# Pooled attention and expert routing on one core: GpSimd's gathers held by one-element copies, weight loads and transposes placed elsewhere in the order

## The chip, the cores and the metric

The kernel runs on one core of one Trainium2 chip. A core has TensorE (PE in the profile), VectorE (DVE), ScalarE (ACT), GpSimd (POOL) and SyncE (SP), each with its own instruction queue, worked off in order. Sixteen DMA engines move data between the off-chip memory and the on-chip buffers; in this kernel GpSimd and SyncE issue all transfers. The metric is the device time of one execution in microseconds (us). Four executions of the kernel before took 259.3, 260.16, 262.19 and 262.2 us; their median is 261.17 us.

## The reference

```python
# q, k, v: (8, 8, 576, 64) f32;  domain_id: 4608 ids of 8 experts;  w1: (8, 512, 1024), w2: (8, 1024, 512) f32
k_p = k.reshape(B, H, 72, 8, D).mean(axis=3);  v_p = v.reshape(B, H, 72, 8, D).mean(axis=3)
attn = softmax(q @ k_p.T / sqrt(D));           x = (attn @ v_p)     # heads joined: x is (4608, 512)
for e in range(8):
    mask = domain_id == e
    out[mask] = np.maximum(x[mask] @ w1[e], 0) @ w2[e]
```

Keys and values are averaged over groups of eight positions, each query attends to the 72 averages, and each of the 4608 resulting rows of 512 numbers goes through the two-layer network of the one expert that its id names.

## The kernel before, in words

**Attention.** The eight batches are worked in four pairs, 0 to 3. For each pair `load_pair` brings in k, q and v (one GpSimd DMA each, f32 in memory and f16 on chip, two buffers per kind). TensorE pools and turns them (`kp_units`, `qt_units`, `vp_units`), `sc_unit` makes the scores of one batch and head (ScalarE takes their exponential out of PSUM), and `av_unit` makes 128 rows of x, which VectorE divides into `x_sb`. After every third `av_unit`, SyncE stores 384 KB of x into the DRAM tensor `x_lin`; there are twelve such stores, three per pair.

**Routing.** In the shadow of the attention the kernel sorts the tokens: each expert has 640 slots, five blocks of 128. `xrow` holds, per slot, the row of `x_lin` to fetch. `gather(e, j)` is one indirect GpSimd DMA of 128 rows into block j of `xg[e % 2]`. For experts 0 and 1 the first three blocks (384 slots, "early") hold only tokens of pairs 0 to 2, so they can be gathered before pair 3 is done; blocks 3 and 4 ("late") need pair 3's rows too.

**Experts.** `turn_units` transposes gathered blocks on TensorE, two blocks at a time, and VectorE copies them to `xT`. `l1_units` gives the eight units of a first layer (ReLU by ScalarE and VectorE in turn, into `hT`), `l2_units` one unit per block of the second layer; each of these ends with a copy to `y` and an indirect GpSimd DMA that scatters 128 rows to `out`. `wload_units(e, which, 1)` is one GpSimd DMA of 2 MB of f32 weights (1 MB on chip): w1 if `which` is 0, w2 if it is 1. Weights of experts 0, 1, 5 and 6 have buffers of their own; the others take the buffers of q, k and v.

**What sets the order.** The order on every engine is written out by hand. While pair p is in work, `put` gives each unit a number, and the list `plan`, sorted by it, is run; 16 numbers make one pair, so pair 3 has 48 to 64. After the plan the calls stand in the order of the code from line 732 on, and `merge` spreads one list between the units of another. [...] GpSimd carries all loads, gathers and scatters in one queue; the framework gives its DMAs eight completion semaphores in rotation, so each DMA on that queue also waits until the one issued eight before it has landed. `nc.values_load` has every engine read the number of overflow blocks into a register, for a branch after the last expert (tokens beyond 640 per expert; there are none in this data).

The names that the change touches: `load_pair` (line 107), the copy after a turned q (493), the plan's weight loads, gathers and turns (710 to 726), the order of the experts (732 to 772). The loads of expert e's two weights are called w1[e] and w2[e] below.

Of the kernel before, what the change touches and what calls it, by code (L numbers as in the profile page):

```python
# [8 lines left out]
F16 = mybir.dt.float16  # L9
# [8 lines left out]
N = B * S  # L18
FF = 1024
E = 8  # L20
# [3 lines left out]
CAP = 640  # L24
NBL = CAP // 128
NBLK = E * NBL
EARLY = 384
# [12 lines left out]
def kernel(  # L40
# [10 lines left out]
    nc = tc.nc  # L51
    const = ctx.enter_context(tc.tile_pool(name="const", bufs=1))
# [51 lines left out]
            return lambda *a, **kw: self.units.append(lambda: getattr(nc.vector, name)(*a, **kw))  # L104

    x_lin = dram.tile([XROWS, HD], F16, name="x_lin")
    def load_pair(t_ap, pr, tag):
        t = wp.tile([128, 72, D], F16, tag=tag, bufs=2, name=tag)
        nc.gpsimd.dma_start(
            t[:].rearrange("p t d -> p (t d)"),  # L110
            t_ap[2 * pr:2 * pr + 2].rearrange("b h (g t) d -> (b h g) (t d)", g=8))
        return t

    with tc.manual_schedule():
# [447 lines left out]
        def wload_units(e, which, parts):  # L562
            box = {}

            def unit(i):
                if i == 0:
                    tag = W_AT[e][which]
                    bufs = 4 if tag == "w" else 2
                    t = wp.tile([128, 4096] if tag == "w" else [128, 72, D], F16, tag=tag, bufs=bufs, name=tag)
                    box["t"] = t[:] if tag == "w" else t[:].rearrange("p t d -> p (t d)")[:, 0:4096]  # L570
                    if which == 0:
                        box["s"] = moe_w1[e].rearrange("(p k) f -> p k f", k=4)
                    else:
# [4 lines left out]
                nc.gpsimd.dma_start(box["t"][:, n * i:n * i + n], box["s"][:, n * i:n * i + n])  # L578
            return [lambda i=i: unit(i) for i in range(parts)]
# [3 lines left out]
        def gather(e, j, rows=XROWS):  # L583
            i = nc.gpsimd.indirect_dma_start(  # L584
                out=xg[e % 2][:, j, :], out_offset=None, in_=x_lin[0:rows, :],
                in_offset=bass.IndirectOffsetOnAxis(ap=xrow[:, NBL * e + j:NBL * e + j + 1], axis=0),
                bounds_check=rows - 1, oob_is_err=False)
            tc.add_to_no_dep_group("xg", i.ins)
# [129 lines left out]

# [26 lines left out]
        u = l1_units(0, EARLY, CAP, h0, 0)  # L745
        g = [lambda j=j: gather(2, j) for j in range(NBL)]
        run(merge(u[:5], g[:3] + count_b()) + [v[2]] + turn_units(1, 3, NBL) + merge(u[5:], g[3:]))
        nblk = nc.values_load(nblk_i[0:1, 0:1], min_val=0, max_val=N // 128)
        h1 = hidden()
        run(l1_units(1, EARLY, CAP, h1, 0))  # L750
        u = l2_units(0, EARLY, CAP, h0) + l2_units(1, EARLY, CAP, h1)
        t = turn_units(2, 0, NBL)
        run([u[0], wload_units(3, 0, 1)[0], t[0], u[1], t[1], u[2], wload_units(3, 1, 1)[0], t[2], u[3]])
        for e in range(2, E):
            h = hidden()
            u = l1_units(e, 0, CAP, h, 0)
            if e == E - 1:
                nc.gpsimd.drain()
            g = []
            if e + 1 < E:  # L760
                g += [lambda j=j: gather(e + 1, j) for j in range(NBL)]
            if e + 2 < E:
                g += wload_units(e + 2, 0, 1)
            run(merge(u, g))
            u = l2_units(e, 0, CAP, h)
            t = turn_units(e + 1, 0, NBL) if e + 1 < E else []
            if e + 2 < E:
                u = u[:1] + wload_units(e + 2, 1, 1) + u[1:]
            n = len(u)
            for i, f in enumerate(t):  # L770
                u.insert(n - 3 + 2 * i, f)
            run(u)

    main.close()

# [110 lines left out]
```

The softmax here doesn't subtract the row's maximum and nothing guards it: scores larger than these inputs give would overflow.

## Time and profile before

| | |
|---|---|
| four executions, us | 259.3, 260.16, 262.19, 262.2 |
| median | 261.17 |
| the profiled execution | 260.09 |
| its span in the profile | 258.4 |
| TensorE busy | 225.9 (87%) |
| VectorE, ScalarE, GpSimd busy | 121.1, 93.1, 108.6 |
| DMA: moved, mean rate | 50.19 MB, 194 GB/s |
| off-chip memory read, written | 67.15 MB, 15.20 MB |

The span runs from the first to the last instruction of one profiled execution; that execution's own time is 1.7 us longer. Times inside the profile count from the span's start. "L578" is line 578 of the kernel. A slice is a fortieth of the span, 6.46 us. DMA is the mean busy share of the sixteen DMA engines; a share above 1 means that packets overlap on an engine. A name such as `k<-in_moe_w_dram` is a weight load into a buffer of tag "k".

### The profile page before, as it was taken

To read this page: it belongs to the slowest core of one execution; us is meant where nothing else is said; L and a number is where in the kernel's file an instruction comes from. 1 tells how busy PE (TensorE), PEld (TensorE's weight loads), DVE (VectorE), ACT (ScalarE), POOL (GpSimd) and SP (SyncE) were. 2 spreads that over 40 slices of the span, in tenths; PEclk is the share of its full clock that TensorE was granted. 3 is DMA by queue.
4 is the path that set the end of the run, shared out by engine and by line. 5 is a ranking of instruction groups with operands and counts; after the bars stand their busy time and mean duration, and the time that the engine had idled before them with its cause. 6 is when DMAs were issued, how large, how long until landed. Compare 5 with 4: busy or idle time off the path is not lost.

```text
span 258.4 us, 4980 instructions
## 1 busy us (share of the span) xinstructions
PE 225.9 (87%) x2048; PEld 144.7 (56%) x2048; DVE 121.1 (47%) x276; ACT 93.1 (36%) x157; POOL 108.6 (42%) x124
## 2 busy tenths in 40 slices
PE   0777989999878469998959999999999999999990
PEld 0555666677556245555735745755756756656640
DVE  7357499696777244443533234333333333343320
ACT  1045657878667614232310420321312312303210
POOL 7002413320000172048745756665756755643052
PEclk9996799999999657999999999999999999999999
DMA  6999999999999969918997999979989989822032
GB/s 106 214 217 217 215 215 228 244 242 243 242 246 261 204 129 243 241 57 146 239 287 164 204 245 205 274 147 219 283 148 193 257 152 190 263 90 100 3 118 81
DMA packets 18153, 50.19 MB, mean 194 GB/s; under 512 B 2316, under 2 KB 10574, under 8 KB 15568
## 3 DMA queue, kind: packets, MB, share of 16 engines
q0 software_dynamic: 16320, 45.10, 80.7%
q1 hardware_dynamic: 1808, 4.76, 5.0%
q8 instruction: 16, 0.26, 0.4%
q14 instruction: 9, 0.07, 0.1%
HBM read 67.15 MB, written 15.20 MB: 319 GB/s over the span
## 4 chain that ended last, share of the span: by engine, by line
PE 41%; DMA 34%; issue 10%; POOL 6%; DVE 5%; POOLq 1%; ACT 0%; DVEq 0%
DMA v<-in_v_dram 19%; PE big L619 10%; PE small L635 9%; DMA xg<-x_lin,xrow 9%; PE wide L635 5%; PE wide L619 5%; DMA out_dram<-y,tok 4%; POOL out_dram L644 4%; PE small L464 3%; PE turn L598 3%; DMA x_lin<-x_sb 2%; PE big L506 2%; DVE x_sb L532 1%; PE big L526 1%; DVE qT L496 1%
## 5 line engine op out<-in xcount | busy, mean ns | idle before, releaser
L584 POOL DMA_INDIRECT xg<-x_lin,xrow x40 | 41.0, 1026 | 63.7 <-DVE x_sb L532 35.9
L644 POOL DMA_INDIRECT out_dram<-y,tok x40 | 40.1, 1004 | 44.4 <-ACT y L642 22.9
L635 PEld LDWEIGHTS <-hT 128*128 128x128 f16 x272 | 25.9, 98 | 26.7
L509 ACT ACTIVATE at<-big 72x576 f16<-72x576 f32 x44 | 28.2, 645 | 20.0 <-PE big L506 19.1
L619 PEld LDWEIGHTS <-w 128*128 128x128 f16 x256 | 24.6, 99 | 11.9 <-issue 2.2
L625 DVE TENSOR_SCALAR hT<-big 128x640 f16<-128x640 f32 (+1 forms) x21 | 15.3, 729 | 27.7 <-PE big L619 24.6
L619 PE MATMUL big<-xT,w 128*128 128x320 f16 (+2 forms) x172 | 28.2, 309 | 0.0
L599 DVE COPY xT<-turn 128x1024 f16<-128x1024 f16 (+1 forms) x24 | 14.4, 598 | 25.3 <-PE turn L598 25.3
L642 ACT ACTIVATE y<-small 128x512 f32<-128x512 f32 x14 | 8.4, 597 | 42.8 <-PE small L635 40.0
L623 ACT ACTIVATE hT<-big 128x640 f16<-128x640 f32 (+1 forms) x21 | 13.2, 628 | 25.9 <-PE big L619 25.9
L598 PE MATMUL turn<-ident,xg 128*128 128x128 f16 x160 | 14.0, 226 | 8.0 <-DMA xg<-x_lin,xrow 8.0
L598 PEld LDWEIGHTS <-xg 128*128 128x128 f16 x160 | 11.0, 100 | 15.0 <-DMA xg<-x_lin,xrow 10.0
L640 DVE COPY y<-small 128x512 f32<-128x512 f32 x13 | 9.0, 692 | 20.1 <-PE small L635 20.1
L635 PE MATMUL small<-w,hT 128*128 128x512 f16 x72 | 17.0, 379 | 0.0
L526 PEld LDWEIGHTS <-at 72*128 72x128 f16 (+1 forms) x320 | 14.0, 105 | 5.3 <-issue 1.5
L506 PE MATMUL big<-qT,kpT 64*72 64x288 f16 x88 | 14.6, 328 | 2.1 <-DVE qT L496 1.7
L532 DVE TENSOR_TENSOR x_sb<-big,rcp 128x512 f16<-128x512 f32 x23 | 15.9, 691 | 0.8
L619 PEld LDWEIGHTS <-k 128*128 128x128 f16 x128 | 12.5, 98 | 5.2
L509 ACT ACTIVATE at<-wide 72x576 f16<-72x576 f32 x20 | 12.9, 646 | 5.5 <-PE wide L506 5.2
L464 PE MATMUL small<-ident,v 128*128 128x128 f16 x144 | 13.5, 243 | 1.6 <-DMA v<-in_v_dram 1.6
L619 PE MATMUL wide<-xT,w 128*128 128x320 f16 (+2 forms) x84 | 13.9, 298 | 0.8 <-DVE y L640 0.8
L625 DVE TENSOR_SCALAR hT<-wide 128x640 f16<-128x640 f32 (+1 forms) x11 | 7.9, 715 | 13.7 <-PE wide L619 13.7
(153 smaller groups left out, 345.2 us busy)
## 6 DMA issues: line engine op xcount, KB each, us to landing
w<-in_moe_w_dram POOLq DMA_DIRECT2D x8, 1024.0 KB, 12.5
k<-in_k_dram POOLq DMA_DIRECT2D x4, 1152.0 KB, 22.6
q<-in_q_dram POOLq DMA_DIRECT2D x4, 1152.0 KB, 22.4
v<-in_v_dram POOLq DMA_DIRECT2D x4, 1152.0 KB, 30.3
x_lin<-x_sb SPq DMA_DIRECT2D x12, 384.0 KB, 11.6
k<-in_moe_w_dram POOLq DMA_DIRECT2D x3, 1024.0 KB, 11.5
v<-in_moe_w_dram POOLq DMA_DIRECT2D x3, 1024.0 KB, 11.6
q<-in_moe_w_dram POOLq DMA_DIRECT2D x2, 1024.0 KB, 9.1
```

The lines of the kernel that those rows point to most:

```text
L464: nc.tensor.matmul(pv[:, i, :], vv[:, o:o + 128], ident[:], start=(t == 0), stop=(t == 3), skip_group_check=True)
L506: nc.tensor.matmul(p[0:72, par, 0:288], s["kpT"][64 * par:64 * par + 64, bh, :], s["qT"][64 * par:64 * par + 64, :, 8 * bh:8 * bh + 8], st ...
L509: nc.scalar.activation(at[0:72, bh % 8, :].rearrange("p (a c) -> p a c", a=2), p[0:72, :, 0:288], AFT.Exp, scale=1.0 / 64.0)
L526: nc.tensor.matmul(pv[r0:r0 + z - a, h, 0:65], s["at", bt][0:72, h, a:z], s["vp"][0:72, 8 * bt + h, :], start=True, stop=True, skip_group_ ...
L532: nc.vector.tensor_tensor(out=x_sb.rearrange("p (b h a) -> p b h a", b=4, h=H), in0=pv[:, :, 0:64].rearrange("p h (a b) -> p b h a", b=4), ...
L584: i = nc.gpsimd.indirect_dma_start(out=xg[e % 2][:, j, :], out_offset=None, in_=x_lin[0:rows, :], in_offset=bass.IndirectOffsetOnAxis(ap=x ...
L598: nc.tensor.transpose(p[:, j - a, kk, :], xg[e % 2][:, j, 128 * kk:128 * kk + 128], ident[:])
L599: nc.vector.tensor_copy(xts[e][:, :, 128 * a:128 * z].rearrange("p k (j c) -> p j k c", c=128), p[:, 0:z - a])
L619: nc.tensor.matmul(p[:, a, 0:m], w1[:, kk, 128 * fi:128 * fi + 128], xT[:, kk, s0 + m * a:s0 + m * a + m], start=(kk == 0), stop=(kk == 3))
L625: nc.vector.tensor_scalar(out=dst, in0=p[:, 0:nh, 0:m], scalar1=0.0, scalar2=None, op0=ALU.max)
L635: nc.tensor.matmul(p, hT[:, fi, 128 * j:128 * j + 128], w2[:, fi, :], start=(fi == 0), stop=(fi == 7))
L644: i = nc.gpsimd.indirect_dma_start(out=out, out_offset=bass.IndirectOffsetOnAxis(ap=orig[0][:, bl:bl + 1], axis=0), in_=y[:], in_offset=No ...
```

## The change

1. `load_pair` can cut a load; q of pair 0 comes in two transfers, of 48 and 24 of its 72 steps. Its fourth turned block goes out by ScalarE instead of VectorE.
2. In the plan, w2[0] moves from behind w1[0] (number 25) to behind the three gathers of expert 0; w1[1] moves from there to behind the three gathers of expert 1, next to w2[1]. The two turns of expert 0's early rows had numbers between 59.5 and 61.5 and now have numbers between 63.6 and 64.8, behind the last scores; its first layer started at 62.0 and now starts at 64.7.
3. After the plan, the four late gathers of experts 0 and 1 no longer stand ahead of everything: three stand between the scatters of expert 0, the fourth behind the first unit of expert 1's first layer. w1[2] moves behind them.
4. `pace` puts a GpSimd copy of one element of `hT`, written by unit `fi` of a first layer, ahead of a gather or a load: GpSimd's queue stops there until that unit has been evicted. Gathers of expert 2 are paced by the late first layers of experts 0 and 1 (and w2[2] by the last unit of expert 0's), and gathers of experts 3 to 7 by units 0, 2, 3, 5, 6 of the first layer before.
5. From expert 2 on, w1 of expert e + 2 is issued after the first second-layer unit of expert e (before: at the end of its first layer), w2 after the third (before: after the first). `values_load` moves from expert 1 to the end of expert 3.

On TensorE the built program differs only where expert 0's early turns stand: two `av_unit`s and three `sc_unit`s now come ahead of them; and in the place of the register load.

```diff
@@ load_pair, first q, qt_units
-    def load_pair(t_ap, pr, tag):
+    def load_pair(t_ap, pr, tag, cuts=(0, 72)):
...
+        src = t_ap[2 * pr:2 * pr + 2].rearrange("b h (g t) d -> (b h g) t d", g=8)
+        for a, z in zip(cuts, cuts[1:]):
+            nc.gpsimd.dma_start(t[:, a:z, :], src[:, a:z, :])
-        qt_[0] = load_pair(q, 0, "q")
+        qt_[0] = load_pair(q, 0, "q", (0, 48, 72))
-                if i == 1:
+                if i == 1 or (pr == 0 and i == 3):
@@ new helpers
+        mark = const.tile([1, 1], F16, name="mark")
+        def pace(hT, fi, c, f):
+            def g():
+                nc.gpsimd.tensor_copy(mark[:], hT[0:1, fi, c:c + 1])
+                f()
+            return g
+        def paced(u, hT, c, fs, at):
+            out_ = []
+            for fi, x in enumerate(u):
+                out_.append(x)
+                out_ += [pace(hT, fi, c, f) for f, i in zip(fs, at) if i == fi]
+            return out_
@@ the plan
-        put(wload_units(0, 0, 1) + wload_units(0, 1, 1), 24.0, 25.0)
+        put(wload_units(0, 0, 1), 24.0, 24.0)
         put([lambda j=j: gather(0, j, XE) for j in range(3)], 54.0, 57.0)
-        put(wload_units(1, 0, 1), 57.1, 57.1)
+        put(wload_units(0, 1, 1), 57.1, 57.1)
         put([lambda j=j: gather(1, j, XE) for j in range(3)], 58.0, 61.0)
-        put(wload_units(1, 1, 1), 61.1, 61.1)
-        put([lambda i=i: run(turn_units_(0, i)) for i in range(2)], 59.5, 61.5)
+        put(wload_units(1, 0, 1) + wload_units(1, 1, 1), 61.1, 61.2)
+        put([lambda i=i: run(turn_units_(0, i)) for i in range(2)], 63.6, 64.8)
-        put([lambda i=i: e0_unit(i) for i in range(8)], 62.0, 69.6)
+        put([lambda i=i: e0_unit(i) for i in range(8)], 64.7, 69.7)
@@ experts 0 to 2
-        for e in range(2):
-            for j in range(3, NBL):
-                gather(e, j)
-        run(wload_units(2, 0, 1))
+        def read_count():
+            nonlocal nblk
+            nblk = nc.values_load(nblk_i[0:1, 0:1], min_val=0, max_val=N // 128)
         u = l2_units(0, 0, EARLY, e0["hT"])
         t = turn_units(1, 0, 3)
-        run([u[0], t[0], u[1], t[1], u[2]])
+        g = [lambda e=e, j=j: gather(e, j) for e in range(2) for j in range(3, NBL)]
+        run([u[0], g[0], t[0], u[1], g[1], t[1], u[2], g[2]])
-        run(merge(l1_units(1, 0, EARLY, he, 0), count_a() + [count_mm]))
-        run(wload_units(2, 1, 1))
+        u = merge(l1_units(1, 0, EARLY, he, 0), count_a() + [count_mm])
+        run(u[:4] + [pace(he, 0, 0, g[3])] + u[4:])
+        run(wload_units(2, 0, 1))
...
-        run(merge(u[:5], g[:3] + count_b()) + [v[2]] + turn_units(1, 3, NBL) + merge(u[5:], g[3:]))
-        nblk = nc.values_load(nblk_i[0:1, 0:1], min_val=0, max_val=N // 128)
+        u = paced(l1_units(0, EARLY, CAP, h0, 0), h0, 0, g[:3] + wload_units(2, 1, 1), [0, 3, 5, 7])
+        run(merge(u[:7], count_b()) + [v[2]] + turn_units(1, 3, NBL) + u[7:])
-        run(l1_units(1, EARLY, CAP, h1, 0))
+        run(paced(l1_units(1, EARLY, CAP, h1, 0), h1, 0, g[3:], [1, 4]))
@@ experts 2 to 7
-            run(merge(u, g))
+            g = [lambda j=j: gather(e + 1, j) for j in range(NBL)] if e + 1 < E else []
+            run(paced(u, h, 0, g, [0, 2, 3, 5, 6]))
...
+            w = wload_units(e + 2, 0, 1) + wload_units(e + 2, 1, 1) if e + 2 < E else [lambda: None] * 2
+            run([u[0], w[0], u[1], t[0], u[2], w[1], t[1], u[3], t[2], u[4]])
+            if e == 3:
+                read_count()
```

More of the change, by code (lines that the diff above doesn't have):

```diff
@@ L106 @@
     x_lin = dram.tile([XROWS, HD], F16, name="x_lin")
-    def load_pair(t_ap, pr, tag):
+    def load_pair(t_ap, pr, tag, cuts=(0, 72)):
         t = wp.tile([128, 72, D], F16, tag=tag, bufs=2, name=tag)
-        nc.gpsimd.dma_start(
-            t[:].rearrange("p t d -> p (t d)"),
-            t_ap[2 * pr:2 * pr + 2].rearrange("b h (g t) d -> (b h g) (t d)", g=8))
+        src = t_ap[2 * pr:2 * pr + 2].rearrange("b h (g t) d -> (b h g) t d", g=8)
+        for a, z in zip(cuts, cuts[1:]):
+            nc.gpsimd.dma_start(t[:, a:z, :], src[:, a:z, :])
         return t
@@ L730 @@
         late = main.enter_context(tc.tile_pool(name="late", bufs=3))
-        for e in range(2):
-            for j in range(3, NBL):
-                gather(e, j)
-        run(wload_units(2, 0, 1))
+        nblk = None
+        def read_count():
+            nonlocal nblk
+            nblk = nc.values_load(nblk_i[0:1, 0:1], min_val=0, max_val=N // 128)
         u = l2_units(0, 0, EARLY, e0["hT"])
         t = turn_units(1, 0, 3)
-        run([u[0], t[0], u[1], t[1], u[2]])
+        g = [lambda e=e, j=j: gather(e, j) for e in range(2) for j in range(3, NBL)]
+        run([u[0], g[0], t[0], u[1], g[1], t[1], u[2], g[2]])
         he = late.tile([128, 8, EARLY], F16, tag="hTl", bufs=1, name="hTe1")
-        run(merge(l1_units(1, 0, EARLY, he, 0), count_a() + [count_mm]))
-        run(wload_units(2, 1, 1))
+        u = merge(l1_units(1, 0, EARLY, he, 0), count_a() + [count_mm])
+        run(u[:4] + [pace(he, 0, 0, g[3])] + u[4:])
+        run(wload_units(2, 0, 1))
         v = l2_units(1, 0, EARLY, he)
@@ L744 @@
         h0 = hidden()
-        u = l1_units(0, EARLY, CAP, h0, 0)
         g = [lambda j=j: gather(2, j) for j in range(NBL)]
-        run(merge(u[:5], g[:3] + count_b()) + [v[2]] + turn_units(1, 3, NBL) + merge(u[5:], g[3:]))
-        nblk = nc.values_load(nblk_i[0:1, 0:1], min_val=0, max_val=N // 128)
+        u = paced(l1_units(0, EARLY, CAP, h0, 0), h0, 0, g[:3] + wload_units(2, 1, 1), [0, 3, 5, 7])
+        run(merge(u[:7], count_b()) + [v[2]] + turn_units(1, 3, NBL) + u[7:])
         h1 = hidden()
-        run(l1_units(1, EARLY, CAP, h1, 0))
+        run(paced(l1_units(1, EARLY, CAP, h1, 0), h1, 0, g[3:], [1, 4]))
         u = l2_units(0, EARLY, CAP, h0) + l2_units(1, EARLY, CAP, h1)
@@ L758 @@
                 nc.gpsimd.drain()
[L759 to L763, printed above, removed]
-            run(merge(u, g))
-            u = l2_units(e, 0, CAP, h)
[L766 to L772, printed above, removed]
+            g = [lambda j=j: gather(e + 1, j) for j in range(NBL)] if e + 1 < E else []
+            run(paced(u, h, 0, g, [0, 2, 3, 5, 6]))
+            u = l2_units(e, 0, CAP, h)
+            t = turn_units(e + 1, 0, NBL) if e + 1 < E else [lambda: None] * 3
+            w = wload_units(e + 2, 0, 1) + wload_units(e + 2, 1, 1) if e + 2 < E else [lambda: None] * 2
+            run([u[0], w[0], u[1], t[0], u[2], w[1], t[1], u[3], t[2], u[4]])
+            if e == 3:
+                read_count()
     main.close()
```

## The prediction, as put on record before the run

> **What bounds the kernel now.** I read the slices first, then the chain of waits in order of time, then TensorE's own timeline, then GpSimd's, and last the landing of single DMAs.
>
> The slices and the chain (start us, length us, what):
>
> ```profile
> PE   0777989999878469998959999999999999999990
> PEclk9996799999999657999999999999999999999999
> DMA  6999999999999969918997999979989989822032
> ...
> 46.71 30.31 DMA v<-in_v_dram
> ...
> 82.25 5.88 DMA x_lin<-x_sb
> ...
> 90.57 2.83 DMA xg<-x_lin,xrow
> ...
> 125.60 9.77 DMA xg<-x_lin,xrow
> ```
>
> Three stages. Up to 77 us the DMA engines are full (9 in every slice), and the chain is one load of v: bytes set the pace. From 77 to 141 us TensorE has dips (slices 14 and 20, counted from 0), and the chain runs through an x_lin store and two gathers. From 141 us TensorE is full. Its timeline shows the dips (start, busy, tile, wait before it in brackets):
>
> ```profile
> 92.11 0.61 PE L598 MATMUL turn<-ident,xg 128*128 128x128 f16 x4 [4.25 <-DMA xg<-x_lin,xrow]
> 93.44 0.61 PE L598 MATMUL turn<-ident,xg 128*128 128x128 f16 x4 [0.72 <-DMA xg<-x_lin,xrow]
> ...
> 121.63 0.60 PE L619 MATMUL wide<-xT,w 128*128 128x256 f16 x4 [0.78 <-DVE y L640]
> ...
> 135.41 0.74 PE L598 MATMUL turn<-ident,xg 128*128 128x128 f16 x8 [2.59 <-DMA xg<-x_lin,xrow]
> ...
> 154.61 0.76 PE L598 MATMUL turn<-ident,xg 128*128 128x128 f16 x8 [0.46 <-DMA xg<-x_lin,xrow]
> ```
>
> All that can be won lies here: 4.25 + 0.72 + 0.78 + 2.59 + 0.46 = 8.8 us, and some of the slow clock around the first wait (PEclk 6, 5, 7; a first-layer unit took 1.39 us at 96.24 against 0.65 at 105.22). The table by stage (PE, PEld, DVE, ACT, POOL busy, clock, DMA share, GB/s) shows that nothing is left later:
>
> ```profile
> 91.00:110.50 19.50, 17.65 (x146) 10.30 (x147) 8.88 (x19) 6.37 (x12) 6.26 (x7) 0.76 0.93 207
> 161.00:180.00 19.00, 19.00 (x130) 11.68 (x128) 6.99 (x10) 4.25 (x7) 11.89 (x13) 1.00 0.97 214
> ```
>
> An expert takes 18.45 us there (169.92 to 188.36 in the chain), and its matmuls alone 8 x 1.09 + 5 x 1.73 + 1.12 = 18.5. The DMA engines are at 0.97: the second bound is close.
>
> **What holds the gathers.** The DMA answers for the issue at 47.97 us (w2[0]), at 82.25 (last store of pair 2) and at 97.52 (w2[1]); the last column is the time to landing:
>
> ```profile
> w<-in_moe_w_dram POOLq DMA_DIRECT2D x1, 1024.0 KB, 43.0
> x_lin<-x_sb SPq DMA_DIRECT2D x1, 384.0 KB, 5.9
> w<-in_moe_w_dram POOLq DMA_DIRECT2D x1, 1024.0 KB, 13.5
> ```
>
> w2[0] lands at 91.0, 15 us before its first use (105.87). It shares the engines with that store, and the first gather (issued 89.14, used 92.11) stands behind it. GpSimd's timeline gives the other mechanism:
>
> ```profile
> 121.70 0.97 POOL L578 DMA_DIRECT2D v<-in_moe_w_dram  x1
> ...
> 134.52 1.02 POOL L584 DMA_INDIRECT xg<-x_lin,xrow  x1 [2.55 <-DMA v<-in_moe_w_dram]
> ```
>
> The gather at 134.52 is the eighth DMA after the w2[2] load at 121.70: the rotation of eight semaphores.
>
> [...] gathers behind a weight load took 9.8 us to landing (issued 125.60), others 2.7 to 2.8[...]. [...] the trace has the clock at half from about 86 to 100 us around the wait. [...] the trace has no one-element copy, its nearest row is a 128x1 memset of 0.10 to 0.12 us.
>
> **The change, part by part.**
>
> *q in two transfers.* It adds one issue (0.6 us, beside queued DMAs) and lets turning begin before all of q is in. The wait it shortens was 0.63 us at 15.89. The set end of this stage is v of pair 3 at 77.06, behind twelve loads in one ring. Gain 0[...]. I take 0. The fourth copy on ScalarE is covered likewise.
>
> *w2[0] out of 81 to 91 us.* In 81 to 88 the engines moved 276 GB/s for the last stores and w2[0]. Without it the last store needs its own time: the small id load took 2.1 us to landing, and 384 KB at 276 GB/s or more is 1.1 to 1.4, so 3.2 instead of 5.9; it lands near 85.4 instead of 88.1. Gathers follow 1.0 us later as before: 86.4, 87.8, 89.1, and land after 2.8 us at 89.2, 90.6, 91.9.
>
> *Scores and two av_units ahead of the turns.* 3 x 0.65 us of ScalarE and 2 x 0.9 of VectorE, alternating in three PSUM buffers, fill TensorE from 87.9 to about 90.8. So it meets gathers that have landed; the waits of 4.97 go. Turns, an av_unit over two batches and another then put the first layer at about 94.5 instead of 96.17, with 1.6 us of work less behind it. Its 8 x 0.65 + 3 x 0.36 = 6.3 us end at 101 with the full clock, at 104 if it stays slow to 100 as before. So expert 0's second layer could start 2 to 5 us sooner than 105.87.
>
> *What is late next: bytes.* w2[0] is issued behind the gathers, at about 90.5, packets from 91.8. Up to w2[1] the ring now holds three weights (3.15 MB) and three gathers (0.39), beside three stores of pair 3 (1.18): 4.7 MB. At 207 / 0.93 = 222 GB/s that is 21.3 us: w2[1] lands at 113.6 (before: 111.0). In order, w2[0] lands about 99.5 (in time), w1[1] about 107 (just in time). Expert 1's second layer therefore starts at 113.6 instead of 116.94: 3.3 us gained, and a fast or slow clock before it changes little. Bounds of this row: 112 if TensorE arrives and 240 GB/s are reached, 115.5 with the slow clock and 205 GB/s.
>
> *From there to expert 2.* Before, 141.84 - 116.94 = 24.9 us, waits of 0.78 and 2.59 in it. The order on TensorE is the same, so 0.78 stays. GpSimd: w1[2] is the eighth DMA after w2[1], so it waits until 113.6; behind it stand the scatters of expert 1, which have their rows only at 115.9, so nobody loses. Then with 1.3 us each: scatters to 119, paced gathers at 120 and 121, scatter, gather at 124.5, w2[2] at 125.8, gathers at 127 and 128.5. The first turn of expert 2 (TensorE at 129.5) has its two blocks: the 2.59 go. Its second turn (131.5) needs the fourth block, which stands behind w2[2]: 5.2 us at 200 GB/s from 127, so 133: a new wait of about 1.8 us (0 to 3). Sum: 113.6 + 24.9 - 2.6 + 1.8 = 137.7, against 141.84: **4.1 us** gained.
>
> *Steady experts.* The 0.46 us at 154.61 go: weights now come after the turn's gathers were long issued. Per expert GpSimd has ten indirect DMAs at 1.32 us, two loads of 1.1 and five copies. I take 0.2 us for a copy (0.1 to 0.5 with its semaphore): 16.4 us of 18.45, covered. If that cover went, each us beyond it costs one per expert. The last paced gather is issued about 10 us after the first layer's start, behind w2 of two experts on; the turn that needs it comes at 16. The tightest pair is issued by 5.2, lands at about 8.5, and is needed at 12.2: 3.7 us of slack. Cost 0 (0 to 2). The register load takes 0.49 us of TensorE's queue wherever it stands, with about 0.16 visible: 0. The tail from the last matmul (252.3) to 258.4 is the same.
>
> Sum: 4.1 + 0.46 = 4.6, with the bound of the clock and of the new wait leaning to more (a fourth block in time gives 6.4): I take 5.0. Against the profiled execution, 260.09 (span 258.4 and 1.7 around it), that is 255.1; the median of four is 1.1 above that execution, so 261.2 - 5.0 = **256.2**.
>
> **Rivals.**
> - *TensorE's waits are the whole price and bytes keep up:* all of 4.97 + 2.59 + 0.46 goes: 253.2. For it: engines idle 0.93 and less between 91 and 121. Against: w2[0] moves into just these gaps.
> - *The bytes bind harder:* w2[1] lands at 115.5 and the new wait is 3: 115.5 + 24.9 - 2.6 + 3 = 140.8, gain 1.5, so 259.7. For it: share 0.97 to 1.05 in steady experts.
> - *Slower: paced gathers land behind w2 in the ring.* Four boundaries (experts 3 to 6) have weight loads behind them in the new order. If the second block lands 3.7 us later than I work out, TensorE begins to wait; at 6.5 us later each boundary costs 2.8, 11.2 in all: 261.2 - 5 + 11.2 = 267.4. For it: the gather at 144.65 took 9.9. Against: there w2[3] had been issued 2.6 us before it; w2 now has 4.5.
> - *It doesn't do what it says:* paced gathers never stop, since GpSimd arrives late anyway. Then the moves of loads alone act, and the time is that of the forecast.
>
> **How the numbers follow.** My forecast 0.58 (its own spread 254.5 to 257.8), all waits gone 0.18, bytes harder 0.18, slower 0.06. About 1% is what a measurement tells from no change: 258.6. Of bytes harder a third lies below it. Faster by over 1%: 0.58 + 0.18 + 0.06 = 0.82; same 0.12; slower 0.06. Leaving out half of the best case's and the last cases' tails, the range is 252.6 to 259.3.
>
> **What would show it.** Right: the store of 82.25 lands in about 3.2 us; no wait at expert 0's turns; w2[0] used soon after it lands; expert 1's second layer at 112 to 115, waiting for w2[1]; a wait of 1 to 2 us at expert 2's second turn; 18.45 us per expert. Wrong if: v of pair 3 lands off 77; turns of experts 3 to 7 wait; the clock falls elsewhere.

## The result, and the profile after

The changed kernel took 262.22 us in the median of 42 runs (260.56 to 266.35), the kernel before 262.18 in 65 runs beside it (258.61 to 264.52): a ratio of 1.0037 with a 95% interval of 1.0018 to 1.0056. Ratios here and below compare the fast runs of the two kernels alone (a run over 1.5% above its kernel's fastest counts as slow), medians are of all runs, so a ratio need not be the quotient of two medians. The forecast of 256.2 us was wrong, and so was its range: of the 5 us nothing arrived. The profiled execution of the changed kernel took 259.57 us, its span is 257.9 (before: 260.09 and 258.4).

The slices of the span, after:

```profile
PE   0788889999788799998947999999999999999990
PEclk9999999999979658999997999999999999999998
DMA  6999999999999299997999879979969979952022
```

The dip of TensorE at slices 13 and 14 is nearly gone (7 and 9 instead of 4 and 6). The slow clock there has not gone with it: slices 13 to 15 read 6, 5, 8, before 6, 5, 7. The dip at slice 20 is deeper (4, and 7 at slice 21), and it now takes a dip of the clock along (7 at slice 21). The hole of the DMA engines has moved from slice 17 (1) to slice 13 (2).

TensorE's timeline (start, busy, tile, wait before it in brackets) at the same places as before, experts 0 to 2:

```profile
91.11 1.03 PE L598 MATMUL turn<-ident,xg 128*128 128x128 f16 x8
...
113.61 1.89 PE L650 MATMUL small<-w,hTe 128*128 128x512 f16 x8
...
118.45 0.60 PE L634 MATMUL wide<-xT,w 128*128 128x256 f16 x4 [0.78 <-DVE y L655]
...
129.41 0.61 PE L598 MATMUL turn<-ident,xg 128*128 128x128 f16 x8
...
136.81 0.61 PE L598 MATMUL turn<-ident,xg 128*128 128x128 f16 x4 [4.84 <-DMA xg<-x_lin,xrow]
137.21 3.24 PE L650 MATMUL small<-w,hT 128*128 128x512 f16 x8
```

No turn of expert 0 waits (before: 4.25 and 0.72), and the first turn of expert 2 stands at 129.41 without a wait (before: 135.41, after 2.59). So at 129.41 the kernel is 6.0 us ahead. Then the second turn of expert 2 waits 4.84 us for a gather, and the second-layer unit behind it takes 3.24 us instead of 1.89. The first layer of expert 2 starts at 142.23 (before: 141.84): everything that was won has been lost within two turns. From there an expert takes 18.45 us as before, and the last one starts at 234.54 (before: 234.84).

The table by stage shows the slow unit (time, then busy time of PE, PEld, DVE, ACT, POOL, then clock, DMA share, GB/s):

```profile
126.00:137.00 11.00, 6.16 (x48) 3.92 (x47) 2.56 (x5) 1.44 (x4) 6.31 (x10) 0.98 1.09 234
137.00:140.30 3.30, 3.30 (x13) 1.39 (x12) 0.69 (x1) 0.00 (x0) 0.00 (x0) 0.56 1.08 226
```

The granted clock falls to 0.56 for the 3.3 us after the wait. The DMA engines are not idle while TensorE waits (1.09): they move something else first. The chain of work that ended last (start, length) says what, and the length of the steps on it:

```profile
82.62 2.77 DMA x_lin<-x_sb
...
117.43 9.43 DMA k<-in_moe_w_dram
127.61 9.15 DMA xg<-x_lin,xrow
136.81 0.61 PE turn L598 x4
```

Last, GpSimd's timeline of the changed kernel:

```profile
117.43 0.62 POOL L578 DMA_DIRECT2D k<-in_moe_w_dram  x1
...
126.31 0.94 POOL L578 DMA_DIRECT2D v<-in_moe_w_dram  x1
127.25 0.18 POOL L609 COPY mark<-hT 1x1 f16<-1x1 f16 x1
127.61 1.05 POOL L584 DMA_INDIRECT xg<-x_lin,xrow  x1 [0.18 <-PE big L634]
```

w1[2] (the buffer k) is issued at 117.43 and lands at 126.86. w2[2] (the buffer v) is issued at 126.31, and the fourth gather of expert 2 at 127.61 behind it, in the same ring (GpSimd's queue of transfers). In this profile every transfer of that queue landed behind those issued ahead of it: w2[2] at 136.42, this gather at 136.76. Between the two loads three gathers and three scatters were issued, so that the ring is far from empty when w2[2] enters it: the last of these gathers, issued at 125.12, landed only at 130.12.

### The profile page after: what moved, and what is told of

Its sections match the earlier page's. It is cut to its first block, busy times and chain, and to the rows that moved or that the text cites. A ratio compares the mean times of both kernels' runs of the same rounds, so it can differ in the third digit from the quotient of the medians.

```text
span 257.9 us, 5042 instructions
## 1 busy us (share of the span) xinstructions
PE 227.3 (88%) x2048; PEld 146.7 (57%) x2048; DVE 121.1 (47%) x275; ACT 94.1 (37%) x158; POOL 115.4 (45%) x157
## 4 chain that ended last, share of the span: by engine, by line
PE 42%; DMA 24%; issue 17%; POOL 9%; DVE 4%; POOLq 1%; ACT 1%; DVEq 0%
DMA q<-in_q_dram 12%; PE big L634 11%; PE small L650 11%; PE wide L634 5%; PE wide L650 5%; DMA k<-in_moe_w_dram 4%; DMA xg<-x_lin,xrow 4%; POOL out_dram L659 3%; DMA out_dram<-y,tok 3%; POOL xg L584 3%; PE turn L598 2%; PE small L492 2%; PE small L214 2%; PE small L435 2%; POOL vc L370 1%
## 5 line engine op out<-in xcount | busy, mean ns | idle before, releaser
L584 POOL DMA_INDIRECT xg<-x_lin,xrow x40 | 41.6, 1039 | 51.8 <-DMA x_lin<-x_sb 38.1
L634 PEld LDWEIGHTS <-w 128*128 128x128 f16 x256 | 25.2, 100 | 12.1 <-issue 2.9
L526 PEld LDWEIGHTS <-at 72*128 72x128 f16 (+1 forms) x320 | 14.8, 109 | 6.3 <-issue 2.9
L650 PE MATMUL small<-w,hT 128*128 128x512 f16 x72 | 18.4, 401 | 0.0
L492 PE MATMUL small<-ident,q 128*128 128x128 f16 x144 | 11.7, 231 | 4.1 <-DMA q<-in_q_dram 2.4
L532 DVE TENSOR_TENSOR x_sb<-big,rcp 128x512 f16<-128x512 f32 x21 | 14.5, 691 | 0.7
L634 PE MATMUL wide<-xT,w 128*128 128x320 f16 (+2 forms) x80 | 13.8, 306 | 0.8 <-DVE y L655 0.8
L640 DVE TENSOR_SCALAR hT<-wide 128x640 f16<-128x640 f32 (+1 forms) x11 | 7.9, 716 | 13.8 <-PE wide L634 13.8
L509 ACT ACTIVATE at<-wide 72x576 f16<-72x576 f32 x19 | 12.3, 645 | 5.2 <-PE wide L506 4.9
```

Source lines behind the costliest of these rows:

```text
L509: nc.scalar.activation(at[0:72, bh % 8, :].rearrange("p (a c) -> p a c", a=2), p[0:72, :, 0:288], AFT.Exp, scale=1.0 / 64.0)
L526: nc.tensor.matmul(pv[r0:r0 + z - a, h, 0:65], s["at", bt][0:72, h, a:z], s["vp"][0:72, 8 * bt + h, :], start=True, stop=True, skip_group_ ...
L532: nc.vector.tensor_tensor(out=x_sb.rearrange("p (b h a) -> p b h a", b=4, h=H), in0=pv[:, :, 0:64].rearrange("p h (a b) -> p b h a", b=4), ...
L584: i = nc.gpsimd.indirect_dma_start(out=xg[e % 2][:, j, :], out_offset=None, in_=x_lin[0:rows, :], in_offset=bass.IndirectOffsetOnAxis(ap=x ...
L634: nc.tensor.matmul(p[:, a, 0:m], w1[:, kk, 128 * fi:128 * fi + 128], xT[:, kk, s0 + m * a:s0 + m * a + m], start=(kk == 0), stop=(kk == 3))
L640: nc.vector.tensor_scalar(out=dst, in0=p[:, 0:nh, 0:m], scalar1=0.0, scalar2=None, op0=ALU.max)
```

## The experiments

Two theories stand against each other. **Place:** the fourth gather stands behind w2[2] in GpSimd's ring; put the load elsewhere and the gain is there. **Bytes:** the engines have too much to move between experts 1 and 4; a wait taken away by moving a load comes back at the next expert. The runs are in four groups, each compared with the kernel before on its own chip: 265.28 us in the first group, 261.99, 262.96 and 262.19 in the others, which are on another chip. The changed kernel was run again, unedited, in groups two, three and four, but not on the chip of the first. Its ratios there are 1.0103, 0.9981 and 0.9984: the same kernel moves by 1.2% between groups, more than its intervals say, so that kernels are compared inside a group only.

### Group one: the place of w2[2], and the copies

`a1_w2_behind`, the changed kernel with w2[2] behind the five gathers of expert 2:

```diff
-        u = paced(l1_units(0, EARLY, CAP, h0, 0), h0, 0, g[:3] + wload_units(2, 1, 1), [0, 3, 5, 7])
+        u = paced(l1_units(0, EARLY, CAP, h0, 0), h0, 0, g[:3], [0, 3, 5])
...
-        run(paced(l1_units(1, EARLY, CAP, h1, 0), h1, 0, g[3:], [1, 4]))
+        run(paced(l1_units(1, EARLY, CAP, h1, 0), h1, 0, g[3:] + wload_units(2, 1, 1), [1, 4, 7]))
```

> The changed kernel, with w2 of expert 2 issued behind the last of expert 2's five gathers instead of ahead of the fourth. Ring theory (the changed kernel gives its gain back because the fourth gather stands behind that load in GpSimd's ring): the wait of 4.84 us at expert 2's second turn falls to under 0.5, the half clock after it goes too (1.5 us), expert 2's first layer starts at about 136.5 instead of 142.4 us, and the time is 5 to 6.5 us under the kernel before: ratio 0.975 to 0.983. Bytes theory (the DMA engines are the bound from here on, whatever the order): the wait comes back at expert 2's second layer or at the turns of expert 3, and the ratio stays at 0.995 to 1.005.

262.51 us, 0.9885 of the kernel before (0.9855 to 0.9915). No turn of expert 2 waits. But the first turn of expert 3 does:

```profile
154.19 0.97 PE L598 MATMUL turn<-ident,xg 128*128 128x128 f16 x8 [3.51 <-DMA xg<-x_lin,xrow]
154.96 3.28 PE L650 MATMUL small<-v,hT 128*128 128x512 f16 x8
```

The gather that it waits for, issued at 141.40, took 12.75 us: w2[2], w1[3] and w2[3] had been issued at 131.82, 134.30 and 138.58, and stood ahead of it. From the first layer of expert 2 to that of expert 3 it is 23.83 us, 5.4 more than 18.45, for a wait of 3.5. So the wait came back at expert 3, as "bytes" had it; the ratio stands between the two expectations.

`a3_w2_halves`, w2[2] in two halves, one ahead of the fourth gather, one behind the fifth:

```diff
+        w = wload_units(2, 1, 2)
-        u = paced(l1_units(0, EARLY, CAP, h0, 0), h0, 0, g[:3] + wload_units(2, 1, 1), [0, 3, 5, 7])
+        u = paced(l1_units(0, EARLY, CAP, h0, 0), h0, 0, g[:3] + w[:1], [0, 3, 5, 7])
...
-        run(paced(l1_units(1, EARLY, CAP, h1, 0), h1, 0, g[3:], [1, 4]))
+        run(paced(l1_units(1, EARLY, CAP, h1, 0), h1, 0, g[3:] + w[1:], [1, 4, 7]))
```

> The changed kernel, with w2 of expert 2 loaded in two halves: one ahead of the fourth gather, one behind the fifth. Ring theory: the fourth gather has half of the load ahead of it, about 3 us less, so the wait at the second turn is 1.5 to 2.2 us instead of 4.84, and the time lies 3 to 4.5 us under the kernel before (ratio 0.983 to 0.989). Bytes theory: no change, ratio 0.995 to 1.005.

259.88 us, 0.9853 (0.9777 to 0.9929). The waits are 0.52 at expert 2 and 1.10 at expert 3, none with a slower clock.

`b1_before_w2_behind`, the same move alone in the kernel before:

```diff
-        run(wload_units(2, 1, 1))
         v = l2_units(1, 0, EARLY, he)
...
         h1 = hidden()
+        run(wload_units(2, 1, 1))
         run(l1_units(1, EARLY, CAP, h1, 0))
```

> The kernel before, with only w2 of expert 2 moved behind the five gathers of expert 2. Ring theory: its 2.59 us wait at expert 2's first turn was the same thing and goes; GpSimd, which came late (gathers from 125.6 us), may leave up to 1 us; time 1.5 to 3 us under before, ratio 0.988 to 0.994. Bytes theory: ratio 1.00.

267.48 us, 1.0048 (1.0019 to 1.0077), which neither theory had. The wait of 2.59 at expert 2's first turn went, but two waits of 2.50 and 0.88 us came ahead of it, in the late first layers of experts 0 and 1, and from expert 3 on each expert took 19.1 us with a wait of 0.4 to 0.5 on `hT`.

`a2_no_copies`, the changed kernel in its order, without the one-element copies:

```diff
             def g():
-                nc.gpsimd.tensor_copy(mark[:], hT[0:1, fi, c:c + 1])
                 f()
```

> The changed kernel without the one-element copies; all orders as they are. Ring theory: around expert 2 GpSimd comes later than the units that it waits for, so nothing moves there, and from expert 3 on TensorE is full either way: within 0.3% of the changed kernel (ratio to before 1.000 to 1.006). A rival, that the copies' waits hold the gathers back and cost the gain: ratio under 0.99 and the wait of 4.84 us shrinks.

267.49 us, 1.0151 (1.0075 to 1.0226), again off both expectations. The wait at expert 2's second turn is still there (4.26), and again an expert takes 19.1 us. On this chip both kernels without copies show 19.1 us and both with them 18.45, so the copies looked like a gain of their own. Groups two and four test that. The kernel before was not profiled on this chip. If it takes 19.1 us per expert there too, five steps of 0.65 us are over 3 us (an estimate from `b1` and `a1`), as much as the 2.8 us by which `a1` is faster, and over half of the 5.4 us of `a3`. The ratios of group one therefore do not show what moving w2[2] is worth; the places of the waits do.

### Group two: the changed kernel again, its parts, and the paces alone

`r1_after` is the changed kernel unedited.

> The changed kernel unedited, as the reference for the runs beside it. Theory 'the wait at expert 2's second turn took the gain': a wait of 4 to 6 us there and the first layer of expert 2 at about 142, 5 to 6 us later than with w2[2] behind the gathers (136.42); ratio to the kernel before 0.997 to 1.005. Rival 'the paced copies are worth 0.6 us per expert on a chip where an expert takes 19.0 without them': the wait is there too, but the ratio is 0.985 to 0.992, since the kernel before loses 3 us in its steady experts on this chip.

262.67 us in 6 runs, 1.0103 (1.0036 to 1.0169). Its wait is 4.59, its first layer of expert 2 at 144.00.

`c1_two_halves_w23_late`: the two halves, the late gathers of expert 0 ahead of its scatters, and w2[3] behind the five gathers of expert 3.

```diff
-        run([u[0], g[0], t[0], u[1], g[1], t[1], u[2], g[2]])
+        run([g[0], g[1], u[0], t[0], u[1], t[1], u[2], g[2]])
...
-        run([u[0], wload_units(3, 0, 1)[0], t[0], u[1], t[1], u[2], wload_units(3, 1, 1)[0], t[2], u[3]])
+        run([u[0], wload_units(3, 0, 1)[0], t[0], u[1], t[1], u[2], t[2], u[3]])
...
-            run(paced(u, h, 0, g, [0, 2, 3, 5, 6]))
+            run(paced(u, h, 0, g + (wload_units(3, 1, 1) if e == 2 else []), [0, 2, 3, 5, 6, 7]))
```

> Three placements on GpSimd: w2[2] in two halves around the fourth and fifth gather of expert 2; two late gathers of expert 0 ahead of its scatters; w2[3] behind the five gathers of expert 3 and not ahead of them. Theory 'gathers stand behind weight loads in the ring': the waits at expert 2's second turn (4.84), at the second-layer buffer near 121 (2.5) and at expert 3's first turn (1.1 to 3.5) all go; 0.970 to 0.980 of the kernel before. Rival 'bytes are the bound and only change places': a wait of 2 us or more appears elsewhere between experts 2 and 4, 0.985 to 0.995.

262.43 us, 1.0102 (1.0046 to 1.0157), the time of the changed kernel beside it. The wait at expert 2's second turn falls from 4.59 to 1.57, its first layer starts at 139.34, 4.7 us before that of `r1_after`, and expert 3 follows after 18.44. But then, at expert 4 (timeline, then stages):

```profile
173.90 0.71 PE L598 MATMUL turn<-ident,xg 128*128 128x128 f16 x8 [3.81 <-DMA xg<-x_lin,xrow]
174.45 3.04 PE L650 MATMUL small<-k,hT 128*128 128x512 f16 x8
```

```profile
170.00:173.90 3.90, 0.09 (x1) 0.00 (x1) 0.69 (x1) 0.00 (x0) 0.30 (x1) 1.00 0.88 282
173.90:177.30 3.40, 3.40 (x17) 1.53 (x18) 0.69 (x1) 0.00 (x0) 2.36 (x3) 0.67 0.62 117
```

w2[3], w1[4] and w2[4], 3 MB, were now issued between 150.33 and 155.81, and the gather of expert 4 issued at 160.81 took 13.04 us behind them. What was won at expert 2 was lost in full two experts later. Both theories allow for that: the bytes are the same, and the edit itself put w2[3] directly ahead of w1[4] and w2[4]. With three places changed at once, this run does not separate them.

`u2_w2_0_ahead`: the plan's weight loads as in the kernel before, the rest changed.

```diff
-        put(wload_units(0, 0, 1), 24.0, 24.0)
+        put(wload_units(0, 0, 1) + wload_units(0, 1, 1), 24.0, 25.0)
-        put(wload_units(0, 1, 1), 57.1, 57.1)
+        put(wload_units(1, 0, 1), 57.1, 57.1)
-        put(wload_units(1, 0, 1) + wload_units(1, 1, 1), 61.1, 61.2)
+        put(wload_units(1, 1, 1), 61.1, 61.1)
```

> The changed kernel with the plan's weight loads as in the kernel before (w2[0] ahead of the gathers, in the way of the last store of pair 2). Theory 'the move of w2[0] gave what was forecast up to expert 1 and the later wait took it': the store takes 5 to 6 us, the first turns wait 0 to 2 us, w2[1] lands 2 us sooner, expert 1's second layer starts within 1.5 us of 113.6 and the wait at expert 2's second turn is 3 to 6 us; within 0.6% of the changed kernel. Rival 'the move of w2[0] is what puts too many bytes between 113 and 136': the wait at expert 2's second turn falls below 2 us and the kernel is 1% faster than the changed one.

262.73 us, 1.0089 (1.0055 to 1.0123). The first turns wait again (1.62 and 1.37), the second layer of expert 1 starts 0.7 us later than in `r1_after` (counted from the last turned v: 117.25 - 84.31 = 32.9 against 115.72 - 83.48 = 32.2), and expert 2's second turn waits 4.71. So the first theory held in the main: with the move of w2[0] the waits near expert 0 go as forecast, at expert 1 it is worth under 1 us, and the later wait is there without it too.

`p1_before_paced`: the kernel before, with copies ahead of the gathers of experts 3 to 7 alone.

```diff
-            run(merge(u, g))
+            run(paced(u, h, 0, g, [0, 2, 3, 5, 6]))
+            if e + 2 < E:
+                run(wload_units(e + 2, 0, 1))
```

> The kernel before with copies ahead of the gathers of experts 3 to 7 alone (units 0, 2, 3, 5, 6), w1 behind the last unit as in the kernel before. Theory 'a burst of five gathers delays the end of each first layer, the pace spreads it': 18.45 us per expert instead of 19.0, ratio 0.986 to 0.992. Rival 'it is where the weights stand that matters': 19.0 per expert stays, ratio 0.997 to 1.003.

261.49 us, 1.0005 (0.997 to 1.004). 18.45 us per expert, as the kernel before has. The paces alone give and cost nothing here.

### Group three: the bytes

`r2_after` is again the changed kernel.

> The changed kernel unedited, beside the three kernels that follow: a wait of 4 to 5 us at expert 2's second turn; 0.998 to 1.012 of the kernel before.

261.98 us, 0.9981 (0.9955 to 1.0007), with a wait of 5.23.

`x1_no_w2_2` moves nothing; it leaves w2[2] out.

```diff
-        u = paced(l1_units(0, EARLY, CAP, h0, 0), h0, 0, g[:3] + wload_units(2, 1, 1), [0, 3, 5, 7])
+        u = paced(l1_units(0, EARLY, CAP, h0, 0), h0, 0, g[:3], [0, 3, 5])
+        wt[2].append(wt[1][1])
```

> The changed kernel without the load of w2[2]: expert 2's second layer computes with w2[1], which is still in its buffer; 1 MB less is moved. Theory 'bytes bind from expert 1 to expert 4, so that a wait taken away without bytes comes back later': no wait at expert 2's second turn, its first layer at 135 to 138, no wait of over 0.6 us at experts 3 and 4 and 18.45 us each, so that the 5 to 6 us stay: 0.975 to 0.983 of the changed kernel. Rival 'only the place of the load matters': the same waits at expert 3 or 4 as with w2[2] behind the gathers (3.5 to 3.8 us), 0.988 to 1.000 of the changed kernel.

255.16 us, 0.9725 (0.9671 to 0.978), 6.8 us under `r2_after`. TensorE's timeline at expert 2:

```profile
130.61 0.61 PE L598 MATMUL turn<-ident,xg 128*128 128x128 f16 x8
...
132.78 0.61 PE L598 MATMUL turn<-ident,xg 128*128 128x128 f16 x8
...
134.96 0.39 PE L598 MATMUL turn<-ident,xg 128*128 128x128 f16 x4
...
136.91 2.34 PE L634 MATMUL big<-xT,k 128*128 128x320 f16 x16
```

Three turns without a wait, 6.30 us from the first to the first layer; in the changed kernel these took 12.82 (129.41 to 142.23). The later experts take 18.70, 18.44 and 19.3 with one wait of 0.54. Nothing is given back: without these bytes the gain stays. With the same bytes in another place (`a1`, `c1`) a wait of 3.5 to 3.8 us returns at a later expert. That fits the theory of bytes. Place counts as well: the next two kernels move every byte and are still 3.7 and 2.5 us faster than `r2_after`. The place decides which turn pays, and how much at once.

`d2_weights_earlier` tries to find the time for those bytes. In 116 to 120 us the changed kernel's engines are at 0.59, because w1[2] stands behind four late gathers, the first of which GpSimd issues only at 109.66, when the last store of x has landed. Here two of them and w1[2] stand ahead of expert 0's scatters, and w2[2] takes w1[2]'s old place:

```diff
-        run([u[0], g[0], t[0], u[1], g[1], t[1], u[2], g[2]])
+        run([g[0], g[1]] + wload_units(2, 0, 1) + [u[0], t[0], u[1], g[2], t[1], u[2]])
...
-        run(wload_units(2, 0, 1))
+        run(wload_units(2, 1, 1))
...
-        u = paced(l1_units(0, EARLY, CAP, h0, 0), h0, 0, g[:3] + wload_units(2, 1, 1), [0, 3, 5, 7])
+        u = paced(l1_units(0, EARLY, CAP, h0, 0), h0, 0, g[:3], [0, 3, 5])
```

> The changed kernel with the same bytes one place earlier: the two late gathers of expert 0, then w1[2], stand ahead of expert 0's scatters, and w2[2] takes w1[2]'s old place behind the fourth late gather, ahead of all gathers of expert 2. Theory 'the engines stand half idle from 116 to 120 us, and those bytes are missing later': the DMA share of 112 to 120 rises from 0.75 to over 0.9, w1[2] lands by 120, w2[2] by 127, no wait at the turns of expert 2 nor of over 0.6 us at 3 and 4; 0.975 to 0.985 of the changed kernel. Rival 'the rate does not rise, the same bytes only come in another order': a wait of 2 us or more at the late turns of experts 0 and 1 (115 to 124) or at expert 3, 0.993 to 1.005.

258.30 us, 0.985 (0.9788 to 0.9911) of the kernel before, 0.987 of the changed kernel (0.985 / 0.9981). The stage from 114 to 120 us, first in `r2_after`, then in this kernel:

```profile
114.00:120.00 6.00, 5.22 (x36) 3.03 (x35) 2.39 (x7) 0.98 (x2) 4.92 (x7) 1.00 0.55 130
```

```profile
114.00:120.00 6.00, 5.81 (x36) 2.94 (x35) 1.96 (x4) 1.39 (x3) 4.78 (x6) 1.00 0.88 159
```

The DMA share rises from 0.55 to 0.88. The waits at expert 2 are now 0.91 and 0.25 at a late turn of expert 1 and 1.16 at its own first turn, none with a slower clock, and expert 3 follows after 18.44. It is nearer to the first theory than to its rival, though 0.987 is just outside what was expected.

`a3b_w2_halves` is the kernel of `a3`, now beside the changed kernel.

> w2[2] in two halves around the fourth and fifth gather of expert 2, as before, now beside the changed kernel on one chip. Theory 'the wait is spread, the bytes stay': waits of 0.3 to 1.5 us at experts 2 and 3, none with the half clock, 0.985 to 0.993 of the changed kernel. Rival 'it is given back in full at expert 3 or 4': 0.997 to 1.003.

259.49 us, 0.9829 (0.9749 to 0.9909); 0.985 of the changed kernel. The waits are 1.70 at expert 2, 1.27 at expert 3 and 0.76 at expert 5, 3.7 us in all against 5.23: most of the wait comes back, but in pieces, and the clock stays up.

### Group four: what was still open

`r3_after` is the changed kernel once more.

> The changed kernel unedited, beside the three kernels that follow: a wait of 4 to 5.5 us at expert 2's second turn; 0.996 to 1.006 of the kernel before, or up to 0.99 on a chip where an expert of the kernel before takes 19 us.

262.33 us, 0.9984 (0.994 to 1.0028); the wait is 4.71.

`u3_turns_first`: the turns and first layer of expert 0 back in their old places.

```diff
-        put([lambda i=i: run(turn_units_(0, i)) for i in range(2)], 63.6, 64.8)
+        put([lambda i=i: run(turn_units_(0, i)) for i in range(2)], 59.5, 61.5)
...
-        put([lambda i=i: e0_unit(i) for i in range(8)], 64.7, 69.7)
+        put([lambda i=i: e0_unit(i) for i in range(8)], 62.0, 69.6)
```

> The changed kernel with expert 0's early turns and first layer at their old places, ahead of the last scores. Theory 'w2[1] sets the start of expert 1's second layer': waits of 1.5 to 3 us at the first turns, second layer of expert 1 within 0.7 us of the changed kernel's and the same wait after it; 0.997 to 1.003 of the changed kernel. Rival 'the cover by scores is what holds expert 1 in time': second layer of expert 1 2 us later or more, 1.006 to 1.012 of the changed kernel.

262.77 us, 1.0048 (1.0017 to 1.0078), which is 1.006 of `r3_after`; the two intervals just overlap. The first turns wait 0.59 and 1.55, as the first theory has it. The second layer of expert 1 does not come later: 115.93 - 84.42 = 31.5 us behind the last turned v, 117.66 - 85.70 = 32.0 in `r3_after`. Its line names the load that it waits for:

```profile
115.93 1.89 PE L650 MATMUL small<-w,hTe 128*128 128x512 f16 x8 [0.57 <-DMA w<-in_moe_w_dram]
...
139.78 0.61 PE L598 MATMUL turn<-ident,xg 128*128 128x128 f16 x4 [5.36 <-DMA xg<-x_lin,xrow]
```

So the scores ahead of the turns take the waits away that the prediction named, and expert 1 does not come sooner for it: here it waits for w2[1], in `r3_after` for w1[1] (1.55 us at 112.27). The place of expert 1 is as the first theory has it; the time is at the lower edge of the rival's range, and why it is not the same stays open.

`a2b_no_copies` is the kernel of `a2`, now beside the changed kernel.

> The changed kernel without the one-element copies, its order kept, beside the changed kernel. Theory 'the copies keep the ends of the first layers in time': 19.0 us per expert with waits of 0.4 to 0.5 on evictions of hT, 1.008 to 1.015 of the changed kernel. Rival 'that was the other chip, and GpSimd arrives late anyway': 18.45 us per expert, 0.997 to 1.004.

262.30 us, 1.0001 (0.997 to 1.0032), the time of `r3_after`. An expert takes 18.45 us, and the wait at expert 2's second turn is 4.28. The copies neither cost nor give anything here, and the wait does not come from them: it is there in the same order without them. What made an expert take 19.1 us on the first chip without copies stays open.

`d3_earlier_and_halves` is `d2` with w2[2] in halves, the second behind the fifth gather.

```diff
-        run(wload_units(2, 1, 1))
+        w = wload_units(2, 1, 2)
+        run(w[:1])
...
-        run(paced(l1_units(1, EARLY, CAP, h1, 0), h1, 0, g[3:], [1, 4]))
+        run(paced(l1_units(1, EARLY, CAP, h1, 0), h1, 0, g[3:] + w[1:], [1, 4, 7]))
```

> Weights one place earlier as in d2, and w2[2] in halves, the second behind the fifth gather of expert 2. Theory 'what d2 has left are places in the ring': the wait at expert 2's first turn (1.16) goes, the others stay; 0.980 to 0.986 of the changed kernel. Rival 'bytes are used up': what is gained there comes back at expert 3, 0.986 to 0.992 as d2.

258.39 us, 0.9876 (0.9818 to 0.9934), as `d2`. The wait at expert 2's first turn is gone and stands at expert 3 (timeline, then the stage behind it):

```profile
152.71 0.75 PE L598 MATMUL turn<-ident,xg 128*128 128x128 f16 x8 [1.86 <-DMA xg<-x_lin,xrow]
153.30 1.89 PE L650 MATMUL small<-v,hT 128*128 128x512 f16 x8
```

```profile
152.70:156.00 3.30, 3.29 (x27) 1.99 (x28) 1.47 (x3) 0.00 (x0) 1.47 (x2) 1.00 0.93 168
```

What was gained at one expert came back at the next, as the rival had it. `a3b`, `d2` and `d3` beat both kernels by 1.1 to 1.7% (six runs each), and the intervals do not tell them apart.

## Why the prediction was wrong

*The stage up to expert 1 held.* The last store of pair 2 took 2.77 us (predicted 3.2). The gathers were issued at 86.31, 87.73 and 89.08 (86.4, 87.8, 89.1). The waits of 4.97 us went. Expert 0's first layer started at 94.32 (94.5) and its second at 102.51 (101 to 104). w1[1] landed at 108.02 (107) and w2[1] at 113.57 (113.6), and expert 1's second layer started at 113.61 (113.6). TensorE has no wait there in this profile, since it reached w2[1] just as that landed; in a repeat it waits for w1[1] just before (1.66 us at 110.45 in `r1_after`). So the loads do set this stage, with nothing to spare, though that the hit is to a hundredth is luck: by the prediction's own figures w2[1] lands at 91.8 + 21.3 = 113.1, and its 116.94 for the kernel before is from the chain, where the timeline has 116.78.

*The slow clock near expert 0 was read as belonging to the wait.* The prediction saw the clock at half "around the wait", and left open whether it would stay. It stayed, with the waits gone (the changed kernel; the last three figures are clock, DMA share, GB/s):

```profile
86.00:94.00 8.00, 7.17 (x80) 5.21 (x80) 5.36 (x13) 4.62 (x8) 6.19 (x6) 0.50 0.48 115
```

In the kernel before the clock fell at 86.5 us, ahead of the wait of 4.25 (87.9 to 92.1), and every profile of these runs has a stretch of 10 to 14 us at half clock that begins between 85 and 92 us. So that wait did not bring it about; what does, no run separates.

*The stage from there to expert 2's first turn held too.* The 0.78 stayed, the 2.59 went, and the turn started at 129.41 (129.5). The issue times were right as well: w2[2] at 126.31 (125.8), the fourth gather at 127.61 (127).

*The step that failed is the "new wait of about 1.8 us (0 to 3)" at expert 2's second turn.* It measured 4.84, and 4.3 to 5.4 in seven more profiles of kernels with this order. The step took "5.2 us at 200 GB/s from 127", as if w2[2] found an empty ring. It did not: w1[2] had taken 9.43 us and landed at 126.86, after w2[2] had been issued, and three gathers and three scatters stood between. The last of these gathers landed at 130.12, so by these landings w2[2] came to the front of the ring 3 us later than was counted; it landed at 136.42, 6.3 us on, not 5.2. The rate was not the fault: 234 GB/s over the 11 us from 126 are 2.6 MB, of which w2[2] is 1.05. The gather took 9.15 us from issue to landing. The profile of before already had the size: a gather behind a weight load took 9.77 us there (issued at 125.60), and the prediction quotes that line without using its length here.

*One term was missing.* At the end of the wait the clock fell to half for about 3.4 us, and the prediction had put that at nothing; its own sign of being wrong, "the clock falls elsewhere", came true. From the first turn of expert 2 to its first layer the changed kernel took 12.82 us against 6.30 in `x1`: 6.5 more, of which 4.84 is the wait and 1.7 the clock. Together the two are 3.0 (4.84 - 1.8) and 1.7 us: 4.7 of the 5.0 us forecast.

*The steady experts held:* 18.45 us, copies of 0.18 us (0.2 taken), and no wait at experts 3 to 7. In the repeats the turns of experts 4 and 5 wait 0.2 to 1.2 us, which shows how close the engines are there; the prediction had allowed 0 to 2. The 0.46 went. *q in two transfers* can't be seen: the last turned v stood at 83.23 against 82.86, and between profiles of this same kernel that time differs by more.

*The rivals.* "The bytes bind harder" named the right resource and the wrong place: it expected w2[1] late, and it bound at w2[2]. It ended at 259.7, because it allowed 3 us for the new wait and nothing for the clock. "Paced gathers land behind w2 in the ring" was priced for experts 3 to 6, where it didn't come true, and not for expert 2, where it did. "Paced gathers never stop" is right in what it comes to: in `a2b` the removal of the copies changes nothing. The time that it gave, the forecast, did not come.

*When the missing term comes* is shown by the runs for some waits. Single waits of 3.51 us (`a1`), 3.81 (`c1`) and 4.84 (the changed kernel) were each followed by about 3.4 us at half clock: the clock was 0.52 over the next 3.4 us in `a1`, 0.67 and 0.82 over the next 3.4 and 3.2 in `c1`, 0.56 from 137.0 to 140.3 in the changed kernel. After those of 1.86 in `d3` and 2.59 in the kernel before it was 1.00. What a single wait between 2.59 and 3.51 us does is not measured here. A wait of 1.8 us, as the prediction took it, would by these runs have cost no clock, so the missing term follows from the mis-sized wait. The length of a single wait does not settle it alone: in `b1` waits of 2.50 and 0.88 us close together were followed by about 3.2 us at half clock too (0.91 in the mean of 131 to 149 us), and near expert 0 the clock was at half where no wait was longer than 0.81.

## What to carry to other kernels

A gather is priced by everything ahead of it in its ring when it is issued, with all that hasn't landed yet, and not by the one load just ahead (the transfers of that queue landed in the order of their issue in the changed kernel's profile, and gathers took 2.1 to 13.04 us in these runs); the nearest measured landing in the profile of before (here 9.77 us) is a good check. Where the DMA engines are as full as here (0.89 to 1.17 from 120 to 138 us in `r2_after`), a wait that goes by moving a load has to be followed to the stages behind, where it can come back (3.51 us in `a1`, 3.81 in `c1`); what held here was moving bytes into time that had been half idle (`d2`, DMA share 0.55 to 0.88) and splitting a load so that no single turn waits long (`a3b`, at most 1.70 us). In these runs several waits under 2 us, well apart (1.70, 1.27 and 0.76 in `a3b`), cost less than one of 3.5 us or more, after which the clock fell (0.52 in `a1`, 0.56 in the changed kernel).

## What the runs showed of the hardware that was not expected

- A long wait costs more than itself: 3.51 us became 5.4 (23.83 - 18.45, `a1`), 3.81 became 5.7 (24.19 - 18.45, `c1`), 4.84 became 6.5 (12.82 - 6.30, the changed kernel against `x1`); a wait of 1.86 cost 2.2 (20.61 - 18.45, `d3`).
- A slow clock does not need a long wait: in every profile it is at half for 10 to 14 us from a point between 85 and 92 us on, with waits of at most 0.81 us just before it (changed kernel), and taking 4.97 us of waits out of that stretch did not end it.
- The landing of one 128 KB gather varied from 2.1 us (the kernel before, issued at 169.13, the last load 13.8 us ahead of it) to 13.04 (three weight loads issued in the 11 us before it, `c1`).
- On one chip two kernels without copies ahead of the gathers took 19.1 us per expert and two with them 18.45; on another chip `a2b`, without them, took 18.45 too. No run tells the cause.
